# Attention with a bucket mask and two dense layers on one core: two weight slots moved out of attention, five heads' sums moved to VectorE, residues moved to GpSimd, and a reordered beginning

## The chip, the core and the metric

The kernel runs on one core of a Trainium2 chip. The core has five engines that run at the same time: TensorE (PE, matrix products into PSUM), VectorE (DVE), ScalarE (ACT), GpSimd (POOL) and SyncE (SP, which here only issues DMAs). An engine takes its instructions strictly in order; engines wait for one another by semaphores. The metric is the device time of one execution in microseconds.

## The reference

```python
# 2 batches, 8 heads, 768 positions, head size 64
q_bucket, k_bucket = the 6 sign bits of q @ proj, k @ proj, as a number
mask = q_bucket[:, :, :, None] == k_bucket[:, :, None, :]
scores = where(mask, (q @ k.T) / 8, -1e9)
attn = exp(scores - max(scores)) / (sum(exp(...)) + 1e-9)
x = (attn @ v), heads side by side          # 1536 tokens x 512
h = x @ w_in                                # 512 -> 2048
x = (h * tanh(softplus(h))) @ w_out         # 2048 -> 512
h = x @ w_in2                               # the second layer
out = (P(h) / (Q(h) + 1e-6)) @ w_out2       # P cubic, Q of |h| and h*h
```

## The kernel before

**Numbers.** Every product of two large matrices is made from three products of rounded numbers: a value is split into its rounded part ("hi", type fp32r) and what is left ("lo", the residue), and hi x hi, hi x lo and lo x hi are added in PSUM. So the kernel is full of casts (`hi`) and subtractions (`lo`) on ScalarE, VectorE and GpSimd. The weights arrive as 64-bit floats and are turned into 32 bits by three integer instructions on VectorE (`bits`), then split.

**Attention.** 16 heads, each in six groups (a key tile of 128 by all 768 queries, one of `NC`). The loop `run` of `attention` walks over 6 x 16 groups; for every group `slot_ops(g)` issues, in the order of the table `order`, each piece of work whose slot is g. In that table `lead` (`smax`) is a score product of a later head for its row maximum: two matrix products on PE and one reduction on VectorE. `st` makes the transposed scores (four products) and their exponential on ScalarE into tile `E[c]`, `pv` multiplies by V once all six tiles are there, and `dsum` sums the exponentials over the keys on PE, by a product with ones. To give PE less to sum, `pair` first adds tiles 0 to 3 on GpSimd (into `sums[h, 0]`); tiles 4 and 5 go to PE as they are. `hi`, `lo`, `move_k`, `move_x` and `move_h` make the split of a head's q and k (buffers `qB`, `qX`, `KK`) several heads ahead, the moves being DMAs on SP's queue. Score banks of PSUM are `S1[0..3]` in the beginning (closed by `upper`) and `T[0..3]`; `two_banks` hands the latter out in turn, and `bound` writes a constant beside the scores.

**Weights in attention.** `EARLY` = 7 of the first layer's 16 weight slots (`w0` to `w6`, each half w_in, half w_out) are converted during attention, in two parts each, one part per head from group `W_AT` = 11 on (`convert` on VectorE, then `slot_split` on ScalarE and GpSimd). The raw q and k of the heads wait in the buffer of slot `EARLY - 1`, two heads at a time (`home`).

**Beginning.** The tuple `start` is an order written out by hand for heads 0 and 1, up to where the loop takes over; `done` keeps the loop from repeating it. `codes` multiplies by the projections, `code_k` and `code_q` turn the signs into rows that add the mask to the score product; `row0` and `row0_copy` put head 0's row maxima into qB; `st0` makes head 0's scores in halves (6 tiles x 2).

**Dense part.** Steps i = 0, 1, ...: each step has `gemm1` of one (token block, slot) and `gemm2` of the one before, 12 products each. `front` is the activation (twice, one of them rounded), `back` the residue of g on VectorE, which `gemm2` needs for its last four products. The slots from `EARLY` on are converted here, in four parts of 256 columns each, spread over steps 1 to 14 (`C1_AT`): `direct_load` (DMA into one of five buffers of `ring[1]`), `direct_bits`, `direct_hi` on ScalarE behind `front`, `direct_lo` on VectorE. In a step VectorE gets the residue of g, then the bit instructions, and last the residues of the weights. The last heads' normalizing (`norm`, `xlo`) also falls into steps 3 to 7.

Of the kernel before, what the change touches and what calls it, by code (L numbers as in the profile page):

```python
# [9 lines left out]
F32 = mybir.dt.float32  # L10
# [3 lines left out]
ACT = mybir.ActivationFunctionType  # L14
ALU = mybir.AluOpType
# [3 lines left out]
B, H, S, D = 2, 8, 768, 64  # L19
NT, DM, DFF = B * S, H * D, 2048  # L20
NF = DFF // 128
NK = DM // 128
HALF = S // 2
# [5 lines left out]
QUAD = S // 4  # L29
OLD = 3  # L30
UP = 124
EARLY = 7
W_AT, W_LEAD = 11, 5
POOL_LO = {("lo", 1): "p", ("lo", 2): "p", ("hi", 2): "p"}
ENG = dict(
    lo="dd", hi="aa", xhi="a", xlo="dd", whi="aaaa", wlo="pppp", vhi="d", vlo="d",
# [13 lines left out]
def attention_moe_moe(ctx: ExitStack, tc: tile.TileContext, kq, v, proj2, cst, eye, w1, w2, ab, out):  # L50
    nc = tc.nc
# [6 lines left out]
    wpool = pool(ctx, "w")  # L58
# [3 lines left out]
    def f32(ap):  # L62
        return ap.bitcast(F32)
# [7 lines left out]
    def lo_pool(o, i, h):  # L71
        nc.gpsimd.tensor_tensor(out=o, in0=i, in1=f32(h), op=ALU.subtract)

    def lo_dve(o, i, h):
        nc.vector.tensor_tensor(out=o, in0=i, in1=f32(h), op=ALU.subtract)  # L75
# [17 lines left out]
    W, raw, scr = {}, {}, {}  # L93
# [25 lines left out]
    def part(l, s):  # L119
        return slice(s * CH[l], (s + 1) * CH[l])  # L120
# [40 lines left out]
    def attention(actx, tctx):  # L161
# [6 lines left out]
        e_p = pool(actx, "pe", 1)  # L168
# [11 lines left out]
        def two_banks():  # L180
            turn[0] += 1
            return T[(turn[0] - 1) % 4]
# [14 lines left out]
        qX = [kq_p.tile([128, S], R32, tag=f"qX{i}", name=f"qX{i}") for i in range(NB)]  # L197
        KK = [kq_p.tile([128, 2, S], R32, tag=f"kk{i}", name=f"kk{i}") for i in range(NB)]
# [36 lines left out]
        raws, home = {}, {}  # L235

        def load(h):
            if not 0 <= h < B * H:
                return
            b, hh = divmod(h, H)  # L240
            raws[h] = home[0][:, h % 2, 0:S]
            nc.sync.dma_start(out=raws[h], in_=kq[b, hh])


        def load0(a):
            if a == 0:
                home[0] = wpool.tile([128, 2, 2 * DM], F32, tag=f"w{EARLY - 1}", name="kq")
                raws[0] = home[0][:, 0, 0:S]
# [20 lines left out]
        def khi0(a):  # L269
            nc.scalar.activation(out=qhalf(KK[0][64:128, 0], a), in_=qhalf(raws[0][0:64], a), func=ACT.Copy)  # L270

        def khi(i):
            o = KK[0][64:128, 1] if i else qX[0][0:64]
            nc.scalar.activation(out=o, in_=raws[0][0:64], func=ACT.Copy)

        def qhi(a):
            nc.vector.tensor_copy(qhalf(qB[0][64:128], a), qhalf(raws[0][64:128], a))
# [154 lines left out]
        def row0(a):  # L432
            p = S1[1 if a else 2]
            for c in range(3 * a, 3 * a + 3):
                nc.tensor.matmul(
                    out=p[0:34, c % 3 * 128:c % 3 * 128 + 128], lhsT=Z[:, 2 * c:2 * c + 34], rhs=I_t,
                    start=True, stop=True,
                )
            return p

        def row0_copy(a, p):
            nc.scalar.activation(out=qhalf(qB[0], a)[32:33], in_=p[32:33, 0:HALF], func=ACT.Copy)
# [4 lines left out]
        def unrow():  # L447
            nc.gpsimd.memset(f32(KK[0])[32:33, 0], 0.0)

        pt = {}  # L450
# [46 lines left out]
        sums = {}  # L497
# [14 lines left out]
        def fold(h, c):  # L512
            nc.vector.tensor_tensor(out=sums[h, 0], in0=sums[h, 0], in1=sums.pop((h, c)), op=ALU.add)

        def whole_sum(h):
            if h == B * H - 1:
                fold(h, 4)

        def dsum(h):
            if not 0 <= h < B * H:  # L520
                return
            parts = [sums.pop((h, 0))] + [pt[h, c] for c in (4, 5) if h < B * H - 1]
            p = two_banks()
            pvt[h, "d"] = p[:, 0]
            for i, e in enumerate(parts):
                for n in range(4):
                    nc.tensor.matmul(  # L527
                        out=pvt[h, "d"][32 * n:32 * n + 32, 0:S // 4], lhsT=ones,
                        rhs=e[:, n // 2, n % 2 * (S // 4):(n % 2 + 1) * (S // 4)], start=(i == 0), stop=(i == len(parts) - 1),
                    )  # L530
# [82 lines left out]
        nh = B * H  # L613
        parts = [(f, s) for f in range(EARLY if wide64 else 0) for s in range(PARTS[0])]
        jobs = {}
# [5 lines left out]
        for n, p in enumerate(parts):  # L621
            i = W_AT + 6 * n
# [14 lines left out]
        def whole(f):  # L637
# [18 lines left out]
            ("code_ka", lambda h: code_k(h, (0,)), -7, 1),  # L656
            ("code_kb", lambda h: code_k(h, (1,)), -7, 1),
            ("quad_k", quad_k, -13, 1),
            ("recip", recip, 17, 0),
            ("lo", lo, -13, 1),  # L660
            ("code_q", code_q, -7, 1),
# [23 lines left out]
        done = set()  # L685
        for name, fn, at, per in order:
            if name == "whole":
                todo = [(at, (f,)) for f in range(EARLY)]
            elif name == "load":
                todo = [(max(at + 6 * h, 6 * (h == OLD + 1)), (h,)) for h in range(nh)]  # L690
            elif name == "lead":
                todo = [(6 * h - 6 + max(c - 3 * (h == 1), 0), (h, c)) for h in range(1, nh) for c in range(per)]
            elif name == "pair":
                todo = [(6 * h + max(c, 1) + (c > 0 and h == nh - 1), (h, c)) for h in range(nh) for c in at[h == nh - 1]]
            elif name in ("quad_in", "quad_in_R"):
                todo = [(at + 6 * h, (h,)) for h in range(nh) if (name == "quad_in_R") == (h % 2 == 1 and h > 3)]
            elif name == "spread":
                todo = [(min(at + 12 * (h // 2), last + 6), (h,)) for h in range(nh)]
            elif type(at) is tuple:
                todo = [(at[c] + 6 * h, (h, c)) for h in range(nh) for c in range(per)]  # L700
            elif per > 0:
                todo = [(at + 6 * h + c, (h, c) if per > 1 else (h,)) for h in range(nh) for c in range(per)]
            elif per == 0:
                todo = [(at + 12 * j, (j,)) for j in range(nh // 2)]
            else:
                todo = [(g, (g,)) for g in range(6 * nh)]
            for g, k in todo:
                slots.setdefault(max(g, 0), []).append((name, fn, k))
# [20 lines left out]
        def coef():  # L729
# [1 line left out]

        start = (
            ("get", 0), ("table",), ("load0", 0), ("load0", 1), ("get", 1), ("load", 1), ("get", 3), ("get", 4), ("get", 2),
            ("warm", 4, True), ("khi0", 0), ("qhi", 0), ("khi0", 1), ("qhi", 1), ("codes", 0), ("code_ka", 0), ("khi", 0),
            ("code_kb", 0), ("code_qa", 0), ("klo",), ("ident",), ("warm", 3, True), ("lead", 0, 0), ("code_qb", 0),
            ("hi", 1), ("lead", 0, 1), ("move_k", 1), ("codes", 1), ("khi", 1), ("qxhi",), ("coef",), ("lo", 1), ("qlo",),
            ("lead", 0, 2), ("warm", 1), ("load_v", 0), ("lead", 0, 3), ("warm", 1), ("move_x", 1), ("load", 3), ("lead", 0, 4),
            ("row0", 0), ("warm", 1), ("code_ka", 1), ("code_kb", 1), ("lead", 0, 5), ("load", 2), ("move_h", 1), ("spare",),
            ("code_qa", 1), ("code_qb", 1), ("st0", 0, 0), ("st0", 1, 0), ("lead", 1, 0), ("st0", 2, 0), ("st0", 3, 0),
            ("row0", 1), ("lead", 1, 1), ("st0", 4, 0), ("lead", 1, 2), ("st0", 5, 0), ("hi", 2), ("lo", 2), ("move_k", 2),  # L740
            ("upper",),
        )

        def run():
            memsets()
            fns = {o[0]: o[1] for o in order}
            fns.update(
                get=get, coef=coef, khi=khi, khi0=khi0, qhi=qhi, qxhi=qxhi, qlo=qlo, klo=klo, row0=lambda a: row0_copy(a, row0(a)),
                ident=ident, spare=spare, st0=st0, load0=load0, table=table, upper=upper,
                code_qa=lambda h: code_q(h, (0,)), code_qb=lambda h: code_q(h, (1,)),  # L750
            )
            done.update((name, (0,)) for name in ("load", "hi", "lo", "move_k", "move_x", "move_h", "fin_b"))
            done.update(("code_q", (h,)) for h in (0, 1))
            for name, *k in start:
                if name == "warm":
                    warm(*k)
                    continue
                done.add((name, tuple(k)))
                fns[name](*k, **({"fn": dict(hi=HI, lo=LO)[name][POOL_LO[name, *k]]} if (name, *k) in POOL_LO else {}))
            for g in range(last):  # L760
                slot_ops(g)
                if g == 5:
                    unrow()

        def tail(i):
            for g in {2: range(last, last + 5), 3: range(last + 5, last + 7), 6: range(last + 7, last + 12),
# [5 lines left out]
    def moe(mctx, tctx, tail):  # L772
# [19 lines left out]
        late_products, halves = [], []  # L792
# [127 lines left out]
        def run():  # L920
# [9 lines left out]
            todo = {}  # L930
# [27 lines left out]

            def direct_lo(f, s):
                r = raw.pop((0, f, s))[:, 0:CH[1]].bitcast(F32)  # L960
                lo_dve(W[0, f][:, 1, part(1, s)], r, W[0, f][:, 0, part(1, s)])

            def split_at(i, l, f, s, lo):
                at(i, slot_hi, l, f, s)
# [2 lines left out]
            for f in range(EARLY, NF):  # L967
                if wide64:
                    for s in range(PARTS[1]):
                        n = PARTS[1] * (f - EARLY) + s  # L970
                        i = spread(n, C1_AT, NF - EARLY)
# [8 lines left out]
            for f in range(NF):  # L980
                for s in range(PARTS[1] if wide64 else 0):
                    n, over = PARTS[1] * f + s, (C_AT, n1 - 2)
                    i = spread(n, over, NF)
# [109 lines left out]
```

## Time and profile before

| | |
|---|---|
| median of 3 runs | 727.5 us (727.35 to 727.51) |
| profiled execution, its own time | 727.7 us |
| its span, first to last instruction | 725.9 us |
| TensorE busy | 720.4 us, 99% of the span |
| VectorE, ScalarE, GpSimd busy | 587.0, 422.3, 112.3 us |
| mean granted TensorE clock | 0.999 |

Busy time counts executing instructions and not waits. Products on TensorE are pipelined, so their modelled ends overlap the next ones, and time between two starts is the better measure. The wait of an engine that does not set the end costs nothing.

### The profile page before, as it was taken

What the parts mean: (1) busy time and instruction counts of PE and PEld (TensorE: products, weight loads), DVE (VectorE), ACT (ScalarE), POOL (GpSimd) and SP (SyncE); (2) the same over time, 40 slices, a digit from 0 to 9 for tenths busy, and PEclk for the clock granted to TensorE, in tenths of its full rate; (3) what the DMA queues carried; (4) which work ended last, traced back from release to release, by engine and by line L of the source; (5) the groups of instructions that cost most, each with busy time, mean ns of one, the idle gap of its engine ahead of it and who ended that gap; (6) DMA issues with size and microseconds to landing.
All of it is one profiled execution on the core that took longest, in us unless ns stands there. A gap on an engine that the chain in (4) does not pass through costs nothing.

```text
span 725.9 us, 11586 instructions
## 1 busy us (share of the span) xinstructions
PE 720.4 (99%) x4173; PEld 575.2 (79%) x4173; DVE 587.0 (81%) x1048; ACT 422.3 (58%) x711; POOL 112.3 (15%) x92
## 2 busy tenths in 40 slices
PE   8999999999999999999999999999999999999998
PEld 5676768686688888888888888888888888888886
DVE  8789999999779885755566876599999888888886
ACT  6767768776653333221132343688887677677674
POOL 7646555564400000000000000000000000000000
PEclk9999999999999999999999999999999999999999
DMA  5787867875143433545447884200001000010001
GB/s 159 188 202 208 228 180 191 216 210 141 35 158 125 133 129 117 158 147 174 138 145 219 264 255 154 88 1 0 1 1 58 1 1 1 1 58 1 1 0 60
DMA packets 48633, 82.50 MB, mean 114 GB/s; under 512 B 6633, under 2 KB 24767, under 8 KB 48575
## 3 DMA queue, kind: packets, MB, share of 16 engines
q1 hardware_dynamic: 48107, 81.55, 38.5%
q8 instruction: 33, 0.54, 0.3%
q10 hardware_dynamic: 468, 0.21, 0.1%
q14 instruction: 25, 0.20, 0.1%
HBM read 55.71 MB, written 14.14 MB: 96 GB/s over the span
## 4 chain that ended last, share of the span: by engine, by line
PE 98%; DVE 1%; DMA 0%; ACT 0%; DVEq 0%; issue 0%
PE h L806 36%; PE y L824 18%; PE y L826 18%; PE s L478 9%; PE s L308 9%; PE s L411 5%; PE s L527 2%; PE s L371 1%; DVE z L415 1%; DMA pr<-proj 0%; PE s L455 0%; PE b L323 0%; PE b L455 0%; DVE kk L350 0%; PE s L323 0%; PE s L344 0%
## 5 line engine op out<-in xcount | busy, mean ns | idle before, releaser
L806 PE MATMUL h<-xh,w 128*128 128x512 f32 x768 | 205.0, 390 | 0.0
L806 PEld LDWEIGHTS h<-xh,w 128*128 128x128 f32 x768 | 144.2, 188 | 30.0 <-PE s L308 0.3
L881 ACT ACTIVATE gh<-h 128x512 fp32r<-128x512 f32 x48 | 28.7, 599 | 166.8 <-PE h L806 153.6
L75 DVE TENSOR_TENSOR gl<-ep,gh 128x512 fp32r<-128x512 f32 x96 | 65.9, 687 | 59.8 <-ACT ep L882 59.1
L806 PE MATMUL h<-xl,w 128*128 128x512 f32 x384 | 102.7, 389 | 0.0
L415 DVE TENSOR_REDUCE smt<-s 128x1 fp32r<-128x770 f32 x90 | 86.0, 959 | 11.5 <-PE s L411 5.6
L826 PE MATMUL y<-w,gh 128*128 128x512 f32 x382 | 95.2, 389 | 0.0
L824 PE MATMUL y<-gh,w 128*128 128x512 f32 x384 | 94.9, 389 | 0.0
L806 PEld LDWEIGHTS h<-xl,w 128*128 128x128 f32 x384 | 72.1, 188 | 14.9
L824 PEld LDWEIGHTS y<-gh,w 128*128 128x128 f32 x384 | 72.1, 188 | 14.9
L826 PEld LDWEIGHTS y<-w,gh 128*128 128x128 f32 x382 | 71.8, 188 | 14.8
L483 ACT ACTIVATE e<-s 128x768 f32<-128x768 f32 x90 | 72.8, 815 | 15.5 <-PE s L478 15.4
L308 PE MATMUL s<-e,vf 128*32 128x386 f32 x768 | 65.3, 488 | 0.0
L888 ACT ACTIVATE ep<-h 128x512 f32<-128x512 f32 x48 | 28.5, 594 | 49.6 <-PE h L806 49.6
L111 DVE SCALAR_TENSOR_TENSOR r<-r,t 128x256 int32<-128x256 int32 (+1 forms) x114 | 52.2, 458 | 5.1 <-DVE t L108 0.5
L108 DVE SCALAR_TENSOR_TENSOR t<-r,t 128x256 int32<-128x256 int32 (+1 forms) x114 | 52.2, 458 | 3.9
L890 DVE TENSOR_TENSOR n<-n,ep 128x512 f32<-128x512 f32 x48 | 33.1, 690 | 25.3 <-ACT n L889 25.3
L411 PE MATMUL s<-kk,qB 128*128 128x384 f32 x192 | 51.9, 352 | 0.2 <-DVE kk L350 0.2
L826 PE MATMUL y<-w,gl 128*128 128x512 f32 x191 | 52.0, 390 | 0.0
L824 PE MATMUL y<-gl,w 128*128 128x512 f32 x192 | 51.4, 389 | 0.0
L503 POOL TENSOR_TENSOR es<-es,e 128x768 f32<-128x768 f32 x30 | 50.8, 1692 | 2.4
L308 PEld LDWEIGHTS s<-e,vf 128*32 128x32 f32 x768 | 25.0, 110 | 32.3 <-issue 30.3
(113 smaller groups left out, 1039.1 us busy)
## 6 DMA issues: line engine op xcount, KB each, us to landing
r<-w SPq DMA_DIRECT2D x100, 256.0 KB
w<-r SPq DMA_DIRECT2D x64, 128.0 KB
w<-w SPq DMA_DIRECT2D x16, 512.0 KB
r<-w SPq DMA_DIRECT2D x14, 512.0 KB
kq<-kq SPq DMA_DIRECT2D x15, 384.0 KB
kk<-qB SPq DMA_DIRECT2D x15, 384.0 KB
vf<-v SPq DMA_DIRECT2D x8, 384.0 KB
R<-d SPq DMA_DIRECT2D x16, 192.0 KB
```

The costliest lines, as they stand in the source:

```text
L75: nc.vector.tensor_tensor(out=o, in0=i, in1=f32(h), op=ALU.subtract)
L108: lambda: nc.vector.scalar_tensor_tensor(out=t, in0=r[:, :, 1], scalar=-0x40000000, in1=t, op0=ALU.bitwise_and, op1=ALU.bitwise_or),
L111: lambda: nc.vector.scalar_tensor_tensor(out=o, in0=r[:, :, 0], scalar=29, in1=t, op0=ALU.logical_shift_right, op1=ALU.bitwise_or),
L308: nc.tensor.matmul(out=o[32 * a:32 * a + 32, 0:HALF + 2], lhsT=w[:, a % 2 * 32:a % 2 * 32 + 32], rhs=x[:, a // 2], start=start, stop=stop,)
L411: nc.tensor.matmul(out=p[:, a, UP:UP + HALF], lhsT=qB[h % NB][:, c * 128:(c + 1) * 128], rhs=qhalf(KK[h % NB][:, 0], a), start=True, stop= ...
L415: nc.vector.tensor_reduce(out=m, in_=p[:, :, UP:UP + HALF + 1], op=ALU.max, axis=AX.XY)
L478: nc.tensor.matmul(out=p[:, a, 0:HALF], lhsT=kk[:, c * 128:(c + 1) * 128], rhs=qq[:, a * HALF:(a + 1) * HALF], start=(i == 0), stop=(i == 1),)
L483: nc.scalar.activation(out=E[c][:, :, 0:HALF], in_=halves(p), func=ACT.Exp, scale=1.0 / D ** 0.5)
L503: nc.gpsimd.tensor_tensor(out=sums[h, 0], in0=sums[h, 0], in1=halves(pt[h, c]), op=ALU.add)
L806: nc.tensor.matmul(out=p, lhsT=w[:, c * 128:(c + 1) * 128], rhs=x[:, c, :], start=(n == 0), stop=(n == 11))
L824: nc.tensor.matmul(out=y[m], lhsT=w[:, DM + m * 128:DM + (m + 1) * 128], rhs=g, **s)
L826: nc.tensor.matmul(out=y[m], lhsT=g[:, m * 128:(m + 1) * 128], rhs=w[:, DM:2 * DM], **s)
```

## The change

Seven things are edited. (1) `EARLY` goes from 7 to 5 and `W_AT` from 11 to 35: attention converts slots w0 to w4 from group 35 on, the last of head 5, one part a head as before, and the dense part converts the 11 others. (2) A new step `light_sum` adds tiles 4 and 5 on VectorE for heads 0 to 4, and `dsum` then takes the sum in place of both. (3) `direct_lo` runs on GpSimd. (4) Heads 2 and 3 get a raw buffer of their own in slot `EARLY - 2`, and their loads stand ahead. (5) The second copy of head 0's hi key rows is made by a DMA (`second`), not by ScalarE; head 1's hi key rows come from ScalarE (`khi`), with `second(1)` in place of `move_k(1)`. (6) The order `start` is changed: `code_q` of head 1 stands ahead of `row0`, `st0(2, 0)` ahead of head 1's first score product, two of head 1's score products move one slot later. (7) `coef` is issued at slot 8.

```diff
-EARLY = 7
-W_AT, W_LEAD = 11, 5
+EARLY = 5
+W_AT, W_LEAD = 35, 5
+LIGHT = 0, 1, 2, 3, 4
...
-            raws[h] = home[0][:, h % 2, 0:S]
+            i = int(h in (2, 3))
+            if i not in home:
+                home[i] = wpool.tile([128, 2, 2 * DM], F32, tag=f"w{EARLY - 1 - i}", name="kq")
+            raws[h] = home[i][:, h % 2, 0:S]
...
-        def khi(i):
-            o = KK[0][64:128, 1] if i else qX[0][0:64]
-            nc.scalar.activation(out=o, in_=raws[0][0:64], func=ACT.Copy)
+        def khi(h):
+            nc.scalar.activation(out=KK[1][64:128, 0] if h else qX[0][0:64], in_=raws[h][0:64], func=ACT.Copy)
+
+        def second(h):
+            nc.sync.dma_start(out=f32(KK[h])[64:128, 1], in_=f32(KK[h])[64:128, 0])
...
+        def light_sum(h):
+            if h in LIGHT:
+                sums[h, 4] = e_p.tile([128, 2, HALF], F32, tag="s4", name="es")
+                nc.vector.tensor_tensor(out=sums[h, 4], in0=halves(pt[h, 4]), in1=halves(pt[h, 5]), op=ALU.add)
...
             parts = [sums.pop((h, 0))] + [pt[h, c] for c in (4, 5) if h < B * H - 1]
+            if h in LIGHT:
+                parts[1:] = [sums.pop((h, 4))]
...
             ("quad_k", quad_k, -13, 1),
+            ("light_sum", light_sum, 5, 1),
             ("recip", recip, 17, 0),
...
-                todo = [(6 * h - 6 + max(c - 3 * (h == 1), 0), (h, c)) for h in range(1, nh) for c in range(per)]
+                todo = [((0, 0, 0, 0, 2, 3)[c] if h == 1 else 6 * h - 6 + c, (h, c)) for h in range(1, nh) for c in range(per)]
...
-            ("warm", 4, True), ("khi0", 0), ("qhi", 0), ("khi0", 1), ("qhi", 1), ("codes", 0), ("code_ka", 0), ("khi", 0),
-            ("code_kb", 0), ("code_qa", 0), ("klo",), ("ident",), ("warm", 3, True), ("lead", 0, 0), ("code_qb", 0),
-            ("hi", 1), ("lead", 0, 1), ("move_k", 1), ("codes", 1), ("khi", 1), ("qxhi",), ("coef",), ("lo", 1), ("qlo",),
-            ("lead", 0, 2), ("warm", 1), ("load_v", 0), ("lead", 0, 3), ("warm", 1), ("move_x", 1), ("load", 3), ("lead", 0, 4),
-            ("row0", 0), ("warm", 1), ("code_ka", 1), ("code_kb", 1), ("lead", 0, 5), ("load", 2), ("move_h", 1), ("spare",),
-            ("code_qa", 1), ("code_qb", 1), ("st0", 0, 0), ("st0", 1, 0), ("lead", 1, 0), ("st0", 2, 0), ("st0", 3, 0),
-            ("row0", 1), ("lead", 1, 1), ("st0", 4, 0), ("lead", 1, 2), ("st0", 5, 0), ("hi", 2), ("lo", 2), ("move_k", 2),
+            ("warm", 4, True), ("khi0", 0), ("qhi", 0), ("khi0", 1), ("qhi", 1), ("second", 0), ("load", 2), ("load", 3),
+            ("codes", 0), ("code_ka", 0), ("khi", 0), ("code_kb", 0), ("code_qa", 0), ("klo",), ("warm", 3, True),
+            ("lead", 0, 0), ("code_qb", 0), ("hi", 1), ("lead", 0, 1), ("codes", 1), ("qxhi",), ("khi", 1), ("lo", 1), ("ident",),
+            ("qlo",), ("lead", 0, 2), ("warm", 1), ("lead", 0, 3), ("warm", 1), ("move_x", 1), ("load_v", 0), ("second", 1),
+            ("lead", 0, 4), ("code_qa", 1), ("code_qb", 1), ("row0", 0), ("warm", 1), ("code_ka", 1), ("code_kb", 1),
+            ("lead", 0, 5), ("move_h", 1), ("spare",), ("st0", 0, 0), ("st0", 1, 0), ("st0", 2, 0),
+            ("lead", 1, 0), ("st0", 3, 0), ("row0", 1), ("lead", 1, 1), ("st0", 4, 0), ("st0", 5, 0), ("lead", 1, 2),
+            ("hi", 2), ("lo", 2), ("move_k", 2),
...
+                if g == 8:
+                    coef()
...
-                lo_dve(W[0, f][:, 1, part(1, s)], r, W[0, f][:, 0, part(1, s)])
+                lo_pool(W[0, f][:, 1, part(1, s)], r, W[0, f][:, 0, part(1, s)])
```

## Rows read from the trace of the kernel before

**Rows 1.** Windows: stretch, its length, busy us (instructions) of each engine, clock, DMA share, GB/s
```profile
120.00:160.00 40.00, 40.00 (x397) 30.34 (x388) 37.34 (x56) 29.51 (x49) 21.28 (x14) 1.00 0.80 210
...
200.00:240.00 40.00, 40.00 (x177) 33.15 (x178) 32.17 (x82) 18.17 (x41) 0.00 (x0) 1.00 0.47 148
```

**Rows 2.** Chain that ended last, 0 to 50 us: start, us, what
```profile
7.46 4.54 DVE z L415 x5
...
18.84 0.50 ACT e L460
...
20.49 1.15 PE s L323 x8
...
21.98 3.89 PE s L308 x48
25.87 0.97 PE s L527 x24
```

**Rows 3.** ScalarE in order of time, 0 to 36: start, us, instruction [idle before <-releaser]
```profile
11.22 0.48 ACT L442 ACTIVATE qB<-b 1x384 fp32r<-1x384 f32 x1 [1.99 <-PE b L435]
11.73 1.18 ACT L359 ACTIVATE qB<-b,cst 14x384 fp32r<-14x384 f32 x2
12.93 0.87 ACT L460 ACTIVATE e<-b 128x384 f32<-128x384 f32 x2
...
17.46 0.49 ACT L460 ACTIVATE e<-s 128x384 f32<-128x384 f32 x1 [0.76 <-PE s L455]
...
21.18 0.17 ACT L462 ACTIVATE s<-ones 128x2 f32<-128x2 f32 x1
```

**Rows 4.** PE in order of time, 0 to 36
```profile
12.08 0.34 PE L455 MATMUL b<-qX,kk 128*128 128x384 f32 x1
```

**Rows 5.** VectorE in order of time, beginning and end of head 1
```profile
14.19 5.40 DVE L415 TENSOR_REDUCE smt<-s 128x1 fp32r<-128x770 f32 x6
...
34.91 1.47 DVE L75 TENSOR_TENSOR qX<-kq,qB 128x768 fp32r<-128x768 f32 x1
36.30 0.41 DVE L105 TENSOR_SCALAR t<-r 128x512 int32<-128x512 int32 x1
...
39.21 6.16 DVE L415 TENSOR_REDUCE smt<-s 128x1 fp32r<-128x770 f32 x6 [1.04 <-PE s L411]
```

**Rows 6.** VectorE in order of time, 128 to 135 and 175 to 183
```profile
130.47 0.95 DVE L594 TENSOR_TENSOR xf<-ev,R 128x768 f32<-128x768 f32 x1
...
175.79 1.82 DVE L594 TENSOR_TENSOR xf<-ev,R 128x768 f32<-128x768 f32 x1
```

**Rows 7.** GpSimd in order of time, 175 to 183
```profile
173.34 3.46 POOL L503 TENSOR_TENSOR es<-es,e 128x768 f32<-128x768 f32 x2
```

**Rows 8.** Lines by form: line, engine, operation, form, count | busy us, mean ns
```profile
L108 DVE SCALAR_TENSOR_TENSOR t<-r,t 128x256 int32<-128x256 int32 x100 | 42.5, 425 | 3.4
...
L506 POOL TENSOR_TENSOR es<-e,e 128x768 f32<-128x768 f32 x16 | 29.7, 1855 | 16.9 <-ACT e L483 16.9
...
L72 POOL TENSOR_TENSOR w<-r,w 128x512 fp32r<-128x512 f32 x13 | 16.8, 1292 | 59.6 <-ACT w L66 59.6
...
L108 DVE SCALAR_TENSOR_TENSOR t<-r,t 128x512 int32<-128x512 int32 x14 | 9.7, 693 | 0.5
```

**Rows 9.** VectorE in order of time, 186 to 290
```profile
204.01 0.69 DVE L75 TENSOR_TENSOR gl<-ep,gh 128x512 fp32r<-128x512 f32 x1 [3.82 <-ACT ep L882]
204.62 0.28 DVE L105 TENSOR_SCALAR t<-r 128x256 int32<-128x256 int32 x1
...
205.86 0.29 DVE L105 TENSOR_SCALAR t<-r 128x256 int32<-128x256 int32 x1
...
218.59 1.21 DVE L75 TENSOR_TENSOR xl<-xf,xh 128x256 fp32r<-128x256 f32 x2 [0.80 <-ACT xh L66]
```

**Rows 10.** PE in order of time, 186 to 240
```profile
207.23 1.07 PE L824 MATMUL y<-gl,w 128*128 128x512 f32 x4
...
212.67 1.07 PE L824 MATMUL y<-gl,w 128*128 128x512 f32 x4
```

More of the change, by code (lines that the diff above doesn't have):

```diff
@@ L747, in run @@
             fns.update(
-                get=get, coef=coef, khi=khi, khi0=khi0, qhi=qhi, qxhi=qxhi, qlo=qlo, klo=klo, row0=lambda a: row0_copy(a, row0(a)),
+                get=get, khi=khi, second=second, khi0=khi0, qhi=qhi, qxhi=qxhi, qlo=qlo, klo=klo, row0=lambda a: row0_copy(a, row0(a)),
                 ident=ident, spare=spare, st0=st0, load0=load0, table=table, upper=upper,
@@ L752, in run @@
             done.update((name, (0,)) for name in ("load", "hi", "lo", "move_k", "move_x", "move_h", "fin_b"))
+            done.add(("move_k", (1,)))
             done.update(("code_q", (h,)) for h in (0, 1))
```

## The prediction

> **What bounds the kernel now.** I read the windows first: busy time per stretch. From 20 us on TensorE (PE) is busy for all of every stretch at a granted clock of 1.00, in attention and in the dense part alike [rows 1]. So a change gains only if it takes work from PE after the beginning, or shortens the beginning, where PE waits; it loses if it makes PE wait where it does not today. Then the chain of work that ended last, for the first 50 us: it leaves PE for VectorE's reductions (4.54 us from 7.46) and for an exponential of ScalarE at 18.84, and from 20.49 on it is PE alone [rows 2]. Then the engines in order of time at the two places the change touches, the beginning [rows 3 to 5] and the first 14 steps of the dense part [rows 9, 10]; last, pairs of instructions of VectorE and GpSimd that overlap [rows 6, 7].
>
> **Light sums.** Today each head but the last sums its denominators on PE from three inputs (the sum of tiles 0 to 3, tile 4, tile 5): 24 instructions in 0.97 us [rows 2], 0.040 each. With `light_sum` heads 0 to 4 have two inputs: 8 instructions fewer, 0.32 us a head, 5 x 0.32 = 1.6 us off PE, which is the bound there. The addition costs VectorE 0.95 us, its cost for an undisturbed 128x768 product [rows 6]. It stands just ahead of the residue of q (34.91 in head 1), and a weight conversion stood just behind that: from 36.30, 0.41 us and twice 0.69 [rows 5, 8], 1.8 us, after which VectorE still idles 1.04 us for PE [rows 5]. With W_AT 35 the first four conversions of attention go, so heads 1 to 4 trade 1.8 us for one sum. It waits for the exponential of tile 5; behind it stand the residue of q, needed two heads later, and the next reductions. The sum is wanted only after the 3.89 us of P times V on PE [rows 2]. If a GpSimd addition holds it up for all of its own 1.7 us (3.46 for two [rows 7]), it takes 2.6, 0.8 us more than the conversion, still inside the 1.04. For head 0, which had no conversion, the cover is the wait of the next reduction for PE. So the waits cost nothing and the term is -1.6 us.
>
> **Beginning.** Up to 12 us nothing changes: the projections, head 0's codes and five reductions keep their order. What changes comes after. In head 1, key rows come from ScalarE (`khi`) in place of a DMA out of qB, so the sign codes of head 1 need not wait for that DMA: they move ahead of the copy of row 0. ScalarE idles 1.99 us before that copy, and the codes take 1.18 [rows 3], so they fit. Today they stand between the copy and the first exponential, which therefore starts at 12.93 although the last of its two products was issued at 12.08 and takes 0.34 [rows 4]; it can start some 0.45 us sooner. From there ScalarE needs 12 exponentials of 0.49 and a copy of 0.48, 6.4 us, but takes until 21.35, the end of the last write to a score bank [rows 3]: 2.0 us of waits, because PE stands in order behind head 1's score products, which wait for reductions. Two of those products move one slot later, and one product of head 0 moves ahead. That can give a few tenths more. The other bound is VectorE: its six reductions of head 1 run back to back from 14.19 to 19.59 [rows 5] and do not move, and the codes of head 2 (20.49 in the chain [rows 2]) use a bank that the last of them frees. So the gain lies between 0 and about 0.8 us; I take 0.6. On SP's queue `second(0)` now waits for the first key cast; behind it stand the loads of heads 2 and 3 (no longer blocked, since they have a slot of their own), `move_x`, and V's load. They are wanted at 20 us, some ten later than they are issued, so I price this, the identity moved past one residue on GpSimd, and the 0.2 us coefficient moved to slot 8 at nothing; V late would delay 21.98 directly.
>
> **Dense part.** Attention converts 5 slots, not 7; the dense part 11, not 9: 44 parts of 256 columns, not 36, over 14 steps. A step is 5.44 us of PE [rows 10]. On VectorE a part's three bit instructions take 1.24 us start to start, the residue of g 0.61 [rows 9]. VectorE also keeps the last heads' work, two pairs of residues at 1.21 [rows 9] and a product at 0.95. Sum after: 44 x 1.24 + 14 x 0.61 + 3.4 = 66.5 of 76.2 us; the weights' residues leave it. Those, 44, go to GpSimd, idle there: 1.29 us for 512 columns, 1.86 for 768 [rows 8], so by a line 0.73 for 256, or 32 us in all. The DMA loads wait for the residue to release one of five buffers; GpSimd does three residues in 2.2 us of a 5.44 us step, so they come as before. Deadlines hold: the last slot's second part is converted in step 14 and wanted in step 15; its residue eight products later.
>
> The question is what the two engines do to each other. A product on VectorE, alone 0.95 us, took 1.82 at 175.79; GpSimd's addition ended at 176.80 and the product 0.81 later [rows 6, 7]: it was held for nearly all of what was left of that addition. So each residue may hold VectorE by some time e. The first thing PE would miss is the residue of g: the first is done at 204.70 and used at 207.23 [rows 9, 10], 2.5 us of slack. The tightest point is step 8, for steps 1 and 8 hold four parts: till its end VectorE has 26 x 1.24 + 8 x 0.61 + 3.4 = 40.5 us to do in 43.5, spare 3.0, with 25 residues: PE waits from e = 5.5 / 25 = 0.22 on. At the end, 43 residues against 9.7 + 2.5 = 12.2: from 0.28. The bounds of e: 0, if the bit instructions are not held as that product was (no row has one beside GpSimd), and 0.73. Between: GpSimd's data time is (1.86 - 1.29) / 256 x 256 = 0.57 us; a bit instruction of 256 takes 0.43 and of 512 0.69 [rows 8], so 0.27 of its 0.46 us start to start is data and 0.19 is not. A residue in the 0.19 that VectorE leaves free, with the 0.14 of start that the product hid (1.01 left, 0.87 lost), costs 0.57 - 0.33 = 0.24. In data time both together need 3.14 x (3 x 0.27 + 0.57) + 0.54 = 4.9 us of 5.44. I take e at 0.2 to 0.25: a loss of 0 to 0.7, and 0 in the sum, since instruction one of the three is shorter.
>
> The Trainium skill (SBUF — State Buffer, Who interferes with whom) says that a VectorE instruction with two SBUF inputs and a GpSimd instruction that reads SBUF exclude each other for the whole instruction. For the product at 175.79 the trace agrees (1.82 for 0.95). By that rule alone, nothing hidden, e is 0.73 and the loss 43 x 0.73 - 12.2 = 19.2 us, against 0 by my reading.
>
> **Sum.** The profiled execution took 727.7 us, 0.2 above the median of 727.5. 727.7 - 1.6 - 0.6 = 725.5; beside the median 725.3.
>
> **Rivals.**
> 1. GpSimd's residues hold VectorE up more than the gaps hide, and PE waits for the residue of g (the other side). For it: every overlap that I find shows the hold [rows 6, 7], and GpSimd always kept its time. Against: the bit instructions have gaps, and are not shown beside GpSimd. It eats the whole gain of 2.2 us at e = (5.5 + 2.2) / 25 = 0.31. With a first residue of a burst at 0.73 - 0.19 and the next ones shorter, e is about 0.43: 43 x 0.43 - 12.2 = 6.3 us lost, 727.5 - 2.2 + 6.3 = 731.6; at 0.54, 736.
> 2. In between, e from 0.25 to 0.37: the loss is 0.7 to 3.7 us and the time 726.0 to 729.0, no change to be told.
> 3. The beginning gives nothing, because VectorE's reductions set it all: 727.5 - 1.6 = 725.9. Speaking for it, those reductions do not move; against, ScalarE's last write stands 1.8 us behind them.
> 4. The light sums do not reach PE's end (late sums make PE wait where it saved): 727.5 - 0.6 = 726.9. Nothing in head 1's cover speaks for it.
>
> **Numbers.** About 0.2% (1.5 us) is what a measurement of this kernel tells from none. Forecast, with rival 3 inside it: 0.54, 724.6 to 726.0. Rival 2 and rival 4: 0.16, 726.0 to 729.0. Rival 1 above 729.0: 0.30, of which 0.14 lies above 732. Faster 0.54, same 0.16, slower 0.30. The range for 8 in 10 is 724.6 to 732.
>
> **What would show it.** Light sums: 16 instructions of 0.65 us in the denominators of heads 0 to 4, and heads 0.32 us shorter than the later ones. Beginning: the first exponential near 12.5, P times V of head 0 near 21.4. Dense part: the bit instructions' mean time on VectorE; if e is small it stays near 0.43, PE's steps stay at 5.44, and the first product of the dense part stands 2.2 us earlier. Steps longer than 5.44 from step 3 or 8 on, with PE waiting for the residue of g, would make me wrong.

## The result and the profile after

The changed kernel takes 734.56 us (median of 4, 734.06 to 735.23) beside 727.42 before (727.30 to 727.51): a ratio of 1.0099, 95% interval 1.0081 to 1.0116. It is slower by 7.1 us, above the range that I gave. The profiled execution took 735.23 us with a span of 733.3.

The windows, as [rows 1]; the third stretch answers to no row of before:

```profile
120.00:160.00 40.00, 40.00 (x376) 30.76 (x376) 37.39 (x56) 29.45 (x48) 22.57 (x14) 1.00 0.82 215
200.00:240.00 40.00, 38.36 (x168) 30.90 (x167) 32.35 (x66) 16.69 (x36) 14.95 (x18) 1.00 0.48 152
240.00:280.00 40.00, 36.22 (x156) 28.31 (x155) 35.99 (x71) 16.02 (x36) 17.21 (x21) 1.00 0.41 134
```

Attention is as full as before. In the dense part PE is idle for 1.6 us of the first forty and 3.8 us of the next, at an unchanged clock, and GpSimd, idle there before, is now busy for 15 and 17 us. Who waits for whom, from 198 to 300 us (total, times, longest; `PEld` is TensorE's loading of weights):

```profile
POOL w L73 <- ACT w L67: 58.9, 43, 11.5
...
PEld y L842 <- DVE gl L76: 8.9, 11, 2.0
...
PE y L842 <- DVE gl L76: 5.4, 5, 1.5
...
DVE t L106 <- DMA r<-w: 1.6, 1, 1.6
...
PE h L824 <- ACT w L67: 0.4, 1, 0.4
```

PE waits for the residue of g (`gl`), as rival 1 had it; before, PE waited for nothing there. The first of these waits, PE in order of time, where [rows 10] had a product every 5.44 us:

```profile
206.00 1.07 PE L842 MATMUL y<-gl,w 128*128 128x512 f32 x4
...
216.88 1.07 PE L842 MATMUL y<-gl,w 128*128 128x512 f32 x4
...
223.58 1.21 PE L842 MATMUL y<-gl,w 128*128 128x512 f32 x4 [1.10 <-DVE gl L76]
...
256.46 1.20 PE L842 MATMUL y<-gl,w 128*128 128x512 f32 x4 [1.03 <-DVE gl L76]
```

The first wait is 1.10 us, and the step 6.70 instead of 5.44. The last row is the ninth of these products, behind the parts of step 8: it comes 50.46 us after the first instead of 8 x 5.44 = 43.52, so 6.9 us are lost by then, at what the prediction called the tightest point. Now the bit instructions and the residues by form, as in [rows 8] (L109 and L112 stand for L108 and L111 of before, L73 for the residue on GpSimd):

```profile
L112 DVE SCALAR_TENSOR_TENSOR r<-r,t 128x256 int32<-128x256 int32 x108 | 55.4, 513 | 6.9
...
L109 DVE SCALAR_TENSOR_TENSOR t<-r,t 128x256 int32<-128x256 int32 x108 | 50.6, 468 | 3.7
L73 POOL TENSOR_TENSOR w<-r,w 128x256 fp32r<-128x256 f32 x44 | 37.2, 846 | 58.9 <-ACT w L67 58.9
L106 DVE TENSOR_SCALAR t<-r 128x256 int32<-128x256 int32 x108 | 31.8, 295 | 3.7 <-DMA r<-w 1.6
```

The two-operand bit instructions went from 425 ns to 468 and 513 on the mean of all 108, of which only 44 have a residue beside them. One such part, VectorE and then GpSimd in order of time:

```profile
258.05 0.29 DVE L106 TENSOR_SCALAR t<-r 128x256 int32<-128x256 int32 x1
258.38 0.42 DVE L109 SCALAR_TENSOR_TENSOR t<-r,t 128x256 int32<-128x256 int32 x1
258.91 0.78 DVE L112 SCALAR_TENSOR_TENSOR r<-r,t 128x256 int32<-128x256 int32 x1
259.72 0.29 DVE L106 TENSOR_SCALAR t<-r 128x256 int32<-128x256 int32 x1
```

```profile
258.55 0.86 POOL L73 TENSOR_TENSOR w<-r,w 128x256 fp32r<-128x256 f32 x1 [1.34 <-ACT w L67]
```

The residue begins at 258.55 while L109 runs. L112 then takes 0.78 us instead of 0.42 and ends 0.28 after the residue. The part takes 1.67 us start to start instead of 1.24: e, the time by which one residue holds VectorE up, is 0.42 us in a row of parts back to back. Of the 44 residues 27 lengthened the third instruction like this and 11 the second. The first instruction, which has one input, is held as well when a residue is already running as it comes up; here it takes 0.79 us instead of 0.29 (VectorE, then GpSimd):

```profile
205.95 0.79 DVE L106 TENSOR_SCALAR t<-r 128x256 int32<-128x256 int32 x1
```

```profile
205.85 1.48 POOL L73 TENSOR_TENSOR w<-r,w 128x256 fp32r<-128x256 f32 x2 [11.52 <-ACT w L67]
```

The rest of the front. The chain of the first 50 us, as [rows 2]:

```profile
12.19 0.50 ACT e L466
...
21.32 3.89 PE s L314 x48
25.20 0.65 PE s L540 x16
```

The first exponential comes at 12.19 instead of 12.93, P times V of head 0 at 21.32 instead of 21.98, and the denominators are 16 instructions in 0.65 us. From head 0 to head 5 the chain takes 57.45 us (to 78.77) instead of 58.87 (21.98 to 80.85): 1.42 us less. But head 5 takes 12.62 us instead of 11.77. It holds the first conversion of attention, and its first instruction on VectorE waited for its load:

```profile
83.50 0.43 DVE L106 TENSOR_SCALAR t<-r 128x512 int32<-128x512 int32 x1 [1.29 <-DMA r<-w]
```

The first dense product comes at 198.60, 1.24 us sooner than before (199.84), where I had forecast 2.2. From there to PE's last product the profile is 8.4 us longer than before.

### The profile page after: what moved, and what is told of

It reads as the page before. It is cut to its first block, busy times and chain, and to the rows that moved or that the text cites. A ratio compares the mean times of both kernels' runs of the same rounds, so it can differ in the third digit from the quotient of the medians.

```text
span 733.3 us, 11670 instructions
## 1 busy us (share of the span) xinstructions
PE 721.2 (98%) x4133; PEld 572.3 (78%) x4133; DVE 596.7 (81%) x1029; ACT 425.6 (58%) x715; POOL 144.6 (20%) x132
## 4 chain that ended last, share of the span: by engine, by line
PE 87%; DVE 9%; issue 2%; DMA 1%; ACT 1%; SPq 0%; DVEq 0%; ACTq 0%
PE h L824 30%; PE y L844 18%; PE y L842 13%; PE s L484 9%; PE s L314 9%; PE s L417 5%; DVE t L109 3%; DVE r L112 2%; PE s L540 2%; DVE t L106 2%; DVE gl L76 1%; PE s L377 1%; DMA r<-w 1%; DMA pr<-proj 0%; PE b L329 0%
## 5 line engine op out<-in xcount | busy, mean ns | idle before, releaser
L73 POOL TENSOR_TENSOR w<-r,w 128x256 fp32r<-128x256 f32 (+1 forms) x53 | 48.8, 922 | 101.0 <-ACT w L67 101.0
L112 DVE SCALAR_TENSOR_TENSOR r<-r,t 128x256 int32<-128x256 int32 (+1 forms) x118 | 62.3, 528 | 7.8
L109 DVE SCALAR_TENSOR_TENSOR t<-r,t 128x256 int32<-128x256 int32 (+1 forms) x118 | 57.5, 487 | 4.1
L67 ACT ACTIVATE w<-r 128x256 fp32r<-128x256 f32 (+1 forms) x53 | 24.1, 454 | 52.3 <-DVE r L112 52.3
```

The costliest lines, as they stand in the source:

```text
L109: lambda: nc.vector.scalar_tensor_tensor(out=t, in0=r[:, :, 1], scalar=-0x40000000, in1=t, op0=ALU.bitwise_and, op1=ALU.bitwise_or),
L112: lambda: nc.vector.scalar_tensor_tensor(out=o, in0=r[:, :, 0], scalar=29, in1=t, op0=ALU.logical_shift_right, op1=ALU.bitwise_or),
```

## The experiments

Each is a small edit of the changed kernel or of the kernel before.

**Residues back on VectorE** (`e1`)

```diff
-                lo_pool(W[0, f][:, 1, part(1, s)], r, W[0, f][:, 0, part(1, s)])
+                lo_dve(W[0, f][:, 1, part(1, s)], r, W[0, f][:, 0, part(1, s)])
```

> The changed kernel with the 44 residues of the weights back on VectorE (one line). Hold theory (each GpSimd residue holds VectorE for about 0.42 us, as the changed kernel's trace suggests, more than the 0.34 us that the residue takes on VectorE itself): no instruction of VectorE is held, bit instructions are back at 0.43 us, and VectorE has 44 x 1.58 + 11.9 = 81.4 us of work against 76.2 and 2.5 of slack; worst at step 8, 26 x 1.58 + 8.3 = 49.4 against 46.0, so 3.4 us are lost, and the time is near 729.5 us, 5 below the changed kernel. Rival, load (two more slots overload the dense part whoever makes the residues): 734 or more, since VectorE gets 15 us of work back. Rival, late release (GpSimd's slower residues free the load buffers late): no loss at all, near 726.

Measured: 731.9 us, ratio 1.0062 (1.0047 to 1.0077). By form, VectorE's bit instructions and its residues:

```profile
L109 DVE SCALAR_TENSOR_TENSOR t<-r,t 128x256 int32<-128x256 int32 x108 | 45.9, 425 | 3.7
...
L76 DVE TENSOR_TENSOR w<-r,w 128x256 fp32r<-128x256 f32 x44 | 15.9, 419 | 0.0
```

The bit instructions are at 425 ns again, so the lengthening belongs to GpSimd's residues. VectorE makes three of its own in a row, and then goes on, in order of time:

```profile
258.71 1.09 DVE L76 TENSOR_TENSOR w<-r,w 128x256 fp32r<-128x256 f32 x3
259.71 0.68 DVE L76 TENSOR_TENSOR gl<-ep,gh 128x512 fp32r<-128x512 f32 x1
```

That is 1.00 us for three, 0.33 each, where GpSimd's residue held it up for 0.42. So the move saved VectorE nothing, and cost the kernel 2.7 us. But the kernel is also 2.4 us slower than the hold theory had it, between that theory and the load theory, and 5.6 us above the fill below. PE's products with `gl`, the first and the ninth, as above:

```profile
206.02 1.07 PE L842 MATMUL y<-gl,w 128*128 128x512 f32 x4
...
254.74 1.21 PE L842 MATMUL y<-gl,w 128*128 128x512 f32 x4 [1.08 <-DVE gl L76]
```

That is 48.72 us instead of 43.52: 5.2 of the 5.6 are lost by the end of step 8. The expectation's own count there was 3.4. VectorE also waited 1.3 us for loads by then (1.8 in all), which had been put at nothing, and its work for the last heads took 4.0 us start to start instead of 3.4 (a reciprocal and the wait behind it were not counted): 5.3. So the load rival was right in part: the two slots more in the dense part cost 5.6 us even when VectorE makes the residues.

**The same move in the kernel before** (`e2`: the edit of `e1` the other way round, in the kernel before; 36 parts)

> The kernel before with its 36 dense residues on GpSimd and nothing else (one line). Hold theory: the hold is there (bit instructions near 0.57 us in the mean) but it fits: up to step 8 VectorE has 21 x 1.24 + 20 x 0.42 + 8.3 = 42.7 us against 46.0, up to step 14 36 x 1.66 + 11.9 = 71.7 against 78.7, so the time stays at 727.5, within 0.5. Late release: the buffers are freed later here too, 729 to 732. Load: 727.5, with bit instructions at 0.43.

Measured: 727.36 us, ratio 1.0002 (0.9992 to 1.0011). By form:

```profile
L108 DVE SCALAR_TENSOR_TENSOR t<-r,t 128x256 int32<-128x256 int32 x100 | 47.5, 475 | 3.4
L111 DVE SCALAR_TENSOR_TENSOR r<-r,t 128x256 int32<-128x256 int32 x100 | 45.9, 459 | 5.9
L105 DVE TENSOR_SCALAR t<-r 128x256 int32<-128x256 int32 x100 | 32.6, 326 | 1.9
```

The hold is there too, on all three instructions (425, 425 and 290 ns in the kernel before), and PE waits for nothing: with 36 parts VectorE has room for it. It takes the two more slots to turn it into a loss.

**GpSimd only writes** (`e3`: the residues of the dense part are not computed; GpSimd fills them with zeros)

```diff
-                r = raw.pop((0, f, s))[:, 0:CH[1]].bitcast(F32)
-                lo_pool(W[0, f][:, 1, part(1, s)], r, W[0, f][:, 0, part(1, s)])
+                raw.pop((0, f, s))
+                nc.gpsimd.memset(f32(W[0, f][:, 1, part(1, s)]), 0.0)
```

> The changed kernel with each GpSimd residue replaced by a fill of the same place with zeros: the residues of slots 5 to 15 of the first layer are left out, nothing else. The fill writes SBUF and reads nothing. Hold theory, the hold being on reading two SBUF operands at once: bit instructions return to 0.43 us, steps to 5.44, and the time is near 726.2 (the 1.2 us won until the dense part stay). If writing alone holds VectorE too, bit instructions stay longer by the fill's 0.25 us or so and the time is between 726 and 730. Load: 734 as before, since the same 44 parts are loaded and converted.

Measured: 726.28 us (725.59 to 727.51), ratio 0.9985 (0.9976 to 0.9995). By form:

```profile
L109 DVE SCALAR_TENSOR_TENSOR t<-r,t 128x256 int32<-128x256 int32 x108 | 46.0, 426 | 3.7
L112 DVE SCALAR_TENSOR_TENSOR r<-r,t 128x256 int32<-128x256 int32 x108 | 45.9, 425 | 4.7
...
L979 POOL MEMSET w<- 128x256 f32 x44 | 11.3, 304 | 37.4 <-DVE xl L76 37.4
```

The bit instructions are at 425 ns again, the steps at 5.44 us throughout, and PE waits for nothing. So the 11 slots fit when nobody makes their residues, and the difference to the changed kernel, 8.3 us, is what the 44 residues cost on GpSimd. In this profile the first dense product stands at 197.50, 2.34 us before that of the kernel before: the front gives what the prediction said when head 5's load comes in time (VectorE waited for none there).

What a fill does to the two-operand bit instructions this run does not show, because the fills wait for nothing that the residues wait for, and none lies beside them. GpSimd, then VectorE, in order of time:

```profile
193.17 9.17 POOL L979 MEMSET w<- 128x256 f32 x36
239.79 2.08 POOL L979 MEMSET w<- 128x256 f32 x8 [37.45 <-DVE xl L76]
```

```profile
196.90 0.95 DVE L607 TENSOR_TENSOR xf<-ev,R 128x768 f32<-128x768 f32 x1
...
240.25 1.77 DVE L106 TENSOR_SCALAR t<-r 128x256 int32<-128x256 int32 x1
```

A product with two inputs beside the fills takes the 0.95 us that it takes alone [rows 6]. The one-input L106, which comes up during the eight fills, takes 1.77 us instead of 0.29 and ends just behind the last of them: writing alone does hold VectorE there. PE waited for nothing all the same.

The Trainium skill (SBUF — State Buffer, Who interferes with whom) says that a VectorE instruction with two SBUF inputs collides with a GpSimd instruction that reads SBUF and not with one that only writes it. The trace agrees on both counts: 0.95 us for the product beside the fills, 0.78 us instead of 0.42 for L112 beside the residue. It also says that the second blocks until the first is through; L112 does end 0.28 us behind the residue. The price of a 0.86 us residue was still only 0.42 us, since it began beside the running L109 and in the gap behind it.

**Each residue twice** (`e5`: the GpSimd line issued twice, same result)

```diff
                 lo_pool(W[0, f][:, 1, part(1, s)], r, W[0, f][:, 0, part(1, s)])
+                lo_pool(W[0, f][:, 1, part(1, s)], r, W[0, f][:, 0, part(1, s)])
```

> The changed kernel with every GpSimd residue issued twice in a row (the second writes the same numbers). Hold theory: two holds of about 0.42 us a part, 43 x 0.42 = 18 us more on VectorE, which already sets the pace: near 752 us, bit instructions longer again. Late release: bit instructions as in the changed kernel, VectorE waiting for loads instead, and 740 to 745, since GpSimd has 44 x 1.7 = 75 us for a stage of 84.

Measured: 751.16 us (one execution), as the hold theory had it; VectorE waited 0.7 us for loads, so late release is not the cause. PE's waits, 198 to 330 us:

```profile
PE y L842 <- DVE gl L76: 16.8, 11, 3.7
```

With none, 44 and 88 residues read by GpSimd: 726.3, 734.6, 751.2 us. The second 44 cost 16.6 us, 0.38 each, with no slack left to take any of it (the dense part of this profile is 16.7 us longer than that of the changed kernel); the first 44 cost 8.3, because the slack took the rest.

**A copy instead of a residue** (`e10`: one operand read; the residues' values are not computed)

```diff
-                lo_pool(W[0, f][:, 1, part(1, s)], r, W[0, f][:, 0, part(1, s)])
+                nc.gpsimd.tensor_copy(W[0, f][:, 1, part(1, s)], r)
```

> The changed kernel with each of the 44 residues of the dense part replaced by GpSimd's copy of the converted chunk: one operand read instead of two, the write as before (the residues' values are not computed). If GpSimd holds VectorE while it reads its operands, one operand holds for about half as long: the bit instructions between 0.43 and 0.47 us on the mean, e near 0.2, and 727 to 730 us. Rival: the hold belongs to two-operand instructions alone: as with the fill, 726.3 us and 0.43 us. Rival: the hold is as long as the instruction, whatever it reads: 732 to 735 us.

Measured: 727.34 us (726.73 to 728.61), ratio 0.9997 (0.9988 to 1.0006). One part and the first instruction of the next, VectorE and GpSimd:

```profile
256.95 0.30 DVE L106 TENSOR_SCALAR t<-r 128x256 int32<-128x256 int32 x1
257.28 0.50 DVE L109 SCALAR_TENSOR_TENSOR t<-r,t 128x256 int32<-128x256 int32 x1
257.91 0.43 DVE L112 SCALAR_TENSOR_TENSOR r<-r,t 128x256 int32<-128x256 int32 x1
...
258.85 0.49 DVE L106 TENSOR_SCALAR t<-r 128x256 int32<-128x256 int32 x1
```

```profile
256.98 0.52 POOL L979 CAST w<-r 128x256 fp32r<-128x256 f32 x1 [0.87 <-DVE r L112]
258.40 0.80 POOL L979 CAST w<-r 128x256 fp32r<-128x256 f32 x1 [0.90 <-DVE r L112]
```

A copy holds VectorE too, and for less: L109 takes 0.50 us instead of 0.43 when the copy starts just behind L106, and L106 takes 0.49 instead of 0.29 in the ten parts where the copy was there first. Start to start such parts take mostly 1.39 and 1.51 us instead of 1.24, so 0.15 to 0.27, and the time lies in the 727 to 730 of the first theory. But the test moved two things: the copy does not wait for ScalarE's cast, so it starts with the part and reaches into L109 by 0.2 us only. Whether one operand holds for less, or only its place was better, stays open. That place counts at all is visible in it.

**First loads a head earlier** (`e4`)

```diff
-            for fn, d in (ring_load, -W_LEAD), (convert, 0), (slot_split, 1):
+            for fn, d in (ring_load, -W_LEAD - 6 * (n < 2)), (convert, 0), (slot_split, 1):
```

> The changed kernel with the loads of the first two weight parts of attention issued one head earlier. In the changed kernel's trace VectorE waits 1.29 us for the first part at 82.2, and head 5 takes 12.6 us instead of 11.8. Late-load theory: this wait goes, head 5 takes 11.8 us again, and the time falls by 0.85 us, to 733.7 (or as much of it as the dense part does not take back). Rival (head 5 is long because VectorE has too much to do there): no change, 734.6.

Measured: 734.14 us (733.84 to 734.40), ratio 1.0093 (1.0076 to 1.0110). VectorE no longer waits for the first part, but head 5 still takes 12.03 us, 0.26 more than the later heads. The median is 0.4 us below that of the changed kernel where 0.85 was expected, and the two intervals overlap, so a gain is not shown. That wait was a side matter.

**The beginning alone** (`e6`: the changed kernel with residues on VectorE and)

```diff
-EARLY = 5
-W_AT, W_LEAD = 35, 5
-LIGHT = 0, 1, 2, 3, 4
+EARLY = 7
+W_AT, W_LEAD = 11, 5
+LIGHT = ()
```

> The kernel before with the new beginning alone (seven slots, no light sums, residues on VectorE). Beginning theory: P times V of head 0 starts at 21.3 us instead of 22.0 and nothing gives it back: 727.35 - 0.65 = 726.7 us. Rival: the loads of heads 2 and 3, which now go out early, or V's load, now later, collide with something and the gain is gone by head 1: 727.3.

Measured: 727.6 us, ratio 1.0002 (0.9993 to 1.0011), not the 726.7 expected. In the trace the gain is there to the end: P times V of head 0 at 21.16, the first dense product at 199.17 (0.67 sooner), PE's last product of the chain done at 721.16 instead of 721.81, and the last output landed at 724.39 instead of 725.05. But from that landing to the end of the span it takes 1.38 us instead of 0.84. More on that below (`e13`).

**The light sums alone** (`e7`: the kernel before with `light_sum` in heads 0 to 4) **and both, with seven slots** (`e8`: as `e6`, with LIGHT 0 to 4)

> The kernel before with the sums of tiles 4 and 5 of heads 0 to 4 on VectorE and nothing else (seven slots, so the conversions of heads 1 to 4 stay too). Room theory: VectorE idled 1.04 us before the first reduction of head 2's successor and needs 0.95 to 1.3 more, so nearly all fits: 5 x 0.30 = 1.5 us won, 725.9. Rival, no room: VectorE, over 9 tenths busy there, gets late with the reductions and PE waits; half or all of the 1.5 us goes, 726.6 to 727.5, and this is what the two slots were moved out for.

> The new beginning and the light sums with seven slots and VectorE's residues, that is the changed kernel without its two edits to the weights. If the parts add up: 727.35 - 0.65 - 1.5 = 725.2 us; with the rival's full VectorE in heads 1 to 4 between 726.0 and 726.8. Either way the dense steps are 5.44 us and PE never waits there, so the 7 us of the change are those two edits alone.

Measured: 727.49 us, ratio 1.0001 (0.9992 to 1.0010), and 728.09 us, ratio 1.0007 (0.9998 to 1.0016). One execution of `e7`, the profiled one, took 730.51 us: a weight load issued at 124.40 took 10.17 us, and VectorE waited 3.16 us for it. The others took at most 728.08. P times V of head 5 begins at 80.90 (80.85 before) in the one and at 80.00 (80.03 in `e6`) in the other: nothing is left of the sums by then. The chain of `e8` says where it went:

```profile
66.56 0.97 DVE smt L421
...
68.91 1.24 DVE es L524
...
70.41 0.81 DVE qX L76
71.22 0.93 DVE xl L76 x2
72.15 0.35 DVE t L106
72.52 0.70 DVE t L109
...
73.93 0.96 DVE smt L421
```

From head 1 on a conversion stands beside the sum (`es`). Heads 1 and 2 still take 11.60 us instead of 11.77, but in heads 3 and 4 (12.03 and 12.32) VectorE has become the bound and PE waits for its reductions. So light sums beside conversions do not keep their gain, contrary to the room that the expectation of `e7` counted on. Taking two slots out of attention bought that room in the change.

**Light sums in two heads ahead of the conversions, seven slots** (`e12`: as `e6`, LIGHT 0 and 1) **and six slots** (`e9`: EARLY 6, W_AT 23, LIGHT 0 to 2, residues on VectorE, first loads early as in `e4`)

> Seven slots in attention as before the change, residues on VectorE, the new beginning, and exponentials added by VectorE in heads 0 and 1 alone, which lie ahead of the conversions. If what took the gain of heads 0 to 4 back was VectorE's lack of room beside conversions, heads 0 and 1 keep 0.64 us: head 5's attention sum starts at 79.4 instead of 80.0 us, and the time is 726.9 us (0.6 below the beginning alone). Rival: VectorE still carries the debt of heads 0 and 1 into head 2 and pays it there: 727.6 us, head 5 at 80.0 us.

> Six slots converted in attention, the first from chunk 23 on, exponentials of heads 0 to 2 added by VectorE, residues on VectorE, the first two slots' loads a head earlier. The light heads have no conversion in them, so they keep 3 x 0.32 us; with the beginning's 0.66 us the first dense product comes at about 198.2 us. Ten slots (40 parts of 1.56 us on VectorE) are left to the dense part. If VectorE keeps up there (steps of 5.44 us throughout, no wait of TensorE for the second gemm's operand), 725.9 to 726.4 us; if the closing part takes back half a us as in the run of the beginning alone, 726.4 to 726.9. Rival: one more slot in the dense part is already too many for VectorE, and TensorE waits there: 728 us or more.

Measured: `e12` 727.53 us (726.78 to 728.89), ratio 1.0003 (0.9994 to 1.0012); `e9` 727.08 us (726.76 to 727.66), ratio 0.9993 (0.9984 to 1.0002). In `e12` head 5 begins at 79.51, as expected for sums that keep their gain, but the time is not the 726.9 expected; 0.4 us is lost in head 7, which took 12.17 us; I did not find why, nor why its times spread over 2 us. In `e9` the first dense product stands at 198.29, 1.55 us sooner than before. With ten slots VectorE all but keeps up; steps 6 to 8 lose 0.4 us together:

```profile
PEld y L842 <- DVE gl L76: 0.6, 2, 0.3
```

The last output of `e9` lands at 723.92, 1.13 us sooner than before, and the end again takes 1.39 us instead of 0.84; the time lies just above the 726.4 to 726.9 expected with such an end.

**Output stores in halves** (`e13`: `e9` and)

```diff
-                    nc.sync.dma_start(out=out[r:r + 128, :], in_=o)
+                    for c in (slice(0, DM // 2), slice(DM // 2, DM)) if t < NBLK - 1 else (slice(0, DM),):
+                        nc.sync.dma_start(out=out[r:r + 128, c], in_=o[:, c])
```

> The kernel with six slots and light sums in heads 0 to 2, with the eight output tiles of the first two blocks stored in two halves each, so that SyncE issues eight transfers more, none of them at the end. In the kernels with the new beginning and residues on VectorE, 0.5 us went between the last transfer's landing and the end of the span (1.38 us instead of 0.84). If that is a pause at a fixed place of SyncE's instructions, eight more of them move it ahead of the end: 1.03 or 0.84 us there, and 726.6 to 726.8 us, 0.1% below the kernel before. Rival: the end of these kernels takes 1.38 us whatever lies ahead of it: 727.1 us again.

Measured: 726.72 us (726.23 to 727.87), ratio 0.9991 (0.9982 to 1.0000). The end takes 1.07 us, and the median is 0.36 below that of `e9`, as a pause at a fixed place of SyncE's instructions would have it; the two intervals overlap. It is the fastest kernel with the whole computation, 0.09% below the kernel before, which is hardly to be told from none.

## Why the prediction was wrong

The step that failed is the size of e: "I take e at 0.2 to 0.25: a loss of 0 to 0.7, and 0 in the sum". Measured, e is 0.42 us part to part, and 0.38 us for each further residue. The rest of that step stood in kind: PE misses the residue of g first, and step 8 is the tightest point. At e = 0.42 the prediction's own count there gives 25 x 0.42 - 5.5 = 5.0 us lost. A load that came 1.6 us late (priced at nothing: "so they come as before") and the last heads' work (4.0 us in `e1`, not 3.4) make it 7.2; the steps show 6.9. Another 0.6 goes in steps 9 to 13 and 0.8 at the last slot's late conversion, 8.4 in the profile and 8.3 between the medians. Rival 1 had the mechanism right, and its price for e, about 0.43; the 6.3 us that it took from the slack of the whole stage was 2 short.

The other half of the same step is the number of parts. With nine slots in the dense part the residues cost nothing on either engine (727.4 us before and in `e2`); with eleven they cost 5.6 us on VectorE (`e1`) and 8.3 on GpSimd. So most of the loss is that VectorE's stage was filled, and the move to GpSimd, meant to make the room, added 2.7.

Why e was too small: I counted the residue's data time against VectorE's gaps (0.19 for each bit instruction and 0.14 of start) as if a residue could use the gaps it likes. The rows show that it begins when ScalarE's cast is done, in most parts in the middle of the second bit instruction, and the third then waits, from 0.42 to 0.78 us. And instruction one of the three, whose shortness was the reason for 0 in the sum, is held too when a residue is already running: once in the changed kernel, seven times in `e2`. I had that hold before me in [rows 6, 7], and set a constructed sum against the one row that showed it.

Point by point:
- **Light sums**, -1.6 forecast: -1.42 by head 5 in the changed kernel, -1.43 in `e3`. Right, at 0.28 a head instead of 0.32, and the waits cost nothing, as [rows 5] said. Rival 4 did not happen in the change; in `e7` and `e8`, with seven slots, it did.
- **Beginning**, -0.6 forecast: -0.66 at P times V of head 0, the first exponential at 12.19. Right in place and size: the three profiles with the old beginning have it at 21.59 to 21.98, the eleven with the new one at 21.00 to 21.32.
- **First load of attention**, priced at nothing without a word: 0.85 us in head 5 of the profiled execution, none in that of `e3`. The five profiles with the same attention code (the changed kernel, `e1`, `e3`, `e5`, `e10`) have head 5 at 11.77 to 12.74 us, so it changes from execution to execution.
- **The residues leave VectorE's sum**, 66.5 of 76.2 us: they don't. Start to start, a part takes VectorE 1.24 + 0.42 = 1.67 us (rounded) with GpSimd's residue and 1.24 + 0.33 = 1.57 when it makes it itself.
- **Sum**: 2.1 us gained in the front less 0.85 at head 5, against 8.3 lost: 7.0 us slower; measured 7.1.

## What to carry to other kernels

Work that is moved from VectorE to GpSimd is not free for VectorE. Where both read SBUF, count the overlap as held time, at the size of the nearest row that shows the hold, until a row of the very pair says less; a one-input instruction is no safe place either (0.79 us instead of 0.29 beside a residue, 1.77 behind eight fills). Compare that with what VectorE needs for the work itself; here the hold was the larger, 0.42 against 0.33, so the idle engine had nothing to give. And before work is put into a stage, write its slack as a number of that work, at the tightest point and not over the whole stage: 5.5 us at step 8 is 13 residues of 0.42, and 25 stood ahead of it.

## What was not expected of the hardware

- The span does not end when the last output has landed. From that landing to the end it took 0.84 to 0.85 us in the kernel before, `e2` and `e7`, 1.03 in the changed kernel, `e1`, `e3`, `e4`, `e5` and `e10`, and 1.38 to 1.39 in `e6`, `e8`, `e9` and `e12`, the same in each kernel of a group. The step from 0.84 to 1.03 is in the traces: at the end SyncE waits for five semaphores in a fixed order, the last landing releases the fifth of them in the first group and the second in the next, and the three waits that are then left take 0.06 us each. In the last group SyncE's closing instructions show a pause of 0.33 us after the landing. Eight more transfers issued much earlier (`e13`) brought 1.39 down to 1.07. That the pause is SyncE fetching its instructions is not shown; that it depends on how many instructions lie ahead rests on this one pair. In `e6` and `e9` it hid about half a microsecond of gain.
- GpSimd is slowed in turn: most residues took 0.85 to 0.87 us beside a busy VectorE and 0.74 where VectorE was idle as it began (at 221.30).
